# Top-k attention and SwiGLU: seven-product gate and value in the last two token blocks

## The chip, the cores and the metric

The kernel runs on one core of a Trainium2 chip. The metric is the device time of one execution in microseconds (us); lower is better. The engines are named as the profile names them: PE (matrix multiply) and PEld (its weight loads), DVE (vector), ACT (scalar), POOL (GpSimd), SP (which only issues DMAs here).

## What is computed

Two stages, all in fp32 (the inputs arrive as float64 for the weights):

```python
# attention: B, H, S, D = 8, 8, 576, 64
scores = q @ k.T / sqrt(D)
kth    = 32nd largest of each row
p      = softmax(where(scores >= kth, scores, -1e9))
x      = (p @ v) as (B*S, H*D) = (4608, 512)
# feed-forward: d_ff = 1536
g   = x @ w_gate                 # 512 -> 1536
val = x @ w_val                  # 512 -> 1536
out = (g * sigmoid(g) * val) @ w_out   # 1536 -> 512
```

## The kernel before, in words

**Attention.** The work of attention is cut into units: a unit is one batch, one tile of 128 query rows (the fifth tile has 64) and a pair of heads. For each unit PE makes the scores (L313, L299) into PSUM, ACT scales them into `sc`, DVE finds the 32 largest by four rounds of MAX8 and MATCH_REPLACE8 (L333, L337), POOL makes the exponent's bias (`shift`, L348), ACT makes the weights (`weigh`, L360 and L365), DVE inverts the sum (L379), and the rows are normalised, one head by ACT (L383) and one by POOL (L385). PE transposes them (`turn`, L399), ACT copies them out (L400), and PE multiplies with the values (`values`, L433), which ACT copies into `xT` (L449), transposed tokens.

**Feed-forward.** The 4608 tokens are cut into 18 blocks of 256 (`BLK`), numbered 0 to 17. Blocks 0 and 1 go another way (`feed_half`, L493, in halves of 128 tokens). For each later block `feed` makes twelve gate and twelve value tiles of 128 rows of d_ff by 256 tokens: four matmuls of 256 moving columns for each tile, one for each 128 of the 512 inputs (`product`, L577). Two tiles share one PSUM bank, of which the feed-forward has three. ACT takes the gate out as tanh(g/2) (L610), g/2 (L611) and adds one (L612), and POOL multiplies the two (L613); the value is copied by ACT (L617) and multiplied in by POOL (L618). The products with `w_out` are already made in the seven-product way from block 1 on: `quarter` (L643) is called seven times for a block, in the order 1, 7, 5, 6, 2, 4, 3, six matmuls of 256 columns each. Between the calls POOL makes the differences and sums of the two token halves of `h` that the next calls take as their stationary operand: `s32` (L650), a sum written into the late half (L658), `s32` again (L663), and the late half once more (L691). For call 7, `s32` of all six early rows must be there; for call 5, the sum of L658, which reads the late halves of all twelve rows. The text of the prediction calls the calls of `quarter` closing products, `s32` the half-differences and L658 the sums of halves.

**Weights.** `weights` is a generator. At each step it does a bit of the loading and rounding of `w_gate`, `w_val` and `w_out` to fp32 (`rounded`), and then, after the plain products of block 0 are done (`plain_done`), of the sums of `w_out` for the seven products (L170 to L186). It is advanced by `rounding`, which is called between DVE's steps of the selection (`dve`).

**Order.** The program's main loop runs over the units and writes the order of every engine's instructions by hand; each engine keeps this order. A generator such as `feed` yields a cost at each piece, and `pieces` calls it as long as a unit has credit, so that feed-forward matmuls stand between those of attention. Work that follows a product is put on two lists, `on_act` and `on_pool`, and written out at the next `flush`. After the last units there is only block 17, without attention beside it. All input loads and output stores are issued from SP, in order, but for three from ACT.

Tiles come from pools with a fixed number of buffers: a new tile takes the buffer that is free, and its first writer waits until the last reader of the old one is done. Those that the change touches: `w` (four buffers of 128 x 1024 x 4 bytes), `xT` (three), `gv` (three, for `half_g`, `val`, `p57`, `p16`), `h` (thirteen), and the three PSUM banks of `ps_f`.

Of the kernel before, what the change touches and what calls it, by code (L numbers as in the profile page):

```python
# [15 lines left out]
P = 128  # L16
# [9 lines left out]
def kernel(  # L26
# [59 lines left out]
    ffn = ctx.enter_context(tc.tile_pool(name="ffn", bufs=2))  # L86
    ps_t = ctx.enter_context(tc.tile_pool(name="ps_t", bufs=5, space=PSUM))
    ps_f = ctx.enter_context(tc.tile_pool(name="ps_f", bufs=3, space=PSUM))

    ident = consts.tile([P, P], FP32, name="ident")  # L90
    make_identity(nc, ident[:])
# [4 lines left out]
        nc.vector.memset(vt[:], 0.0)  # L96
        vlast.append(vt)
    wg = consts.tile([P, KC, DFF], FP32, name="wg")
    wv = consts.tile([P, KC, DFF], FP32, name="wv")
    wo = consts.tile([P, MC, DM], FP32, name="wo")  # L100

    def rounded(src, dst):
# [21 lines left out]
    def weights():  # L124


        pieces = []
        for f in range(0, DFF, WP):
            for src, dst in ((w_gate, wg), (w_val, wv)):
                for c in range(0, KC, 2):  # L130
                    rows = src[c * P : (c + 2) * P, f : f + WP]
                    pieces.append((
                        rows.rearrange("(c p) f -> p c f", p=P), dst[:, c : c + 2, f : f + WP]
                    ))
        for c in range(MC):
            pieces.append((
                w_out[c * P : (c + 1) * P].rearrange("p (c f) -> p c f", c=2),
                wo[:, c].rearrange("p (c f) -> p c f", c=2),
            ))
        pieces = [rounded(*p) for p in pieces]  # L140
        step = [0] * len(pieces)

        def upto(i, k):

            while 0 <= i < len(pieces) and step[i] < k:
                next(pieces[i], None)
                step[i] += 1


        lags = (5, 2, 0)  # L150
        for n in range(2 * len(pieces) + 4):
            for k, lag in enumerate(lags):
                if (n - lag) % 2 == 0:
                    upto((n - lag) // 2, len(lags) - k)
            ready[0] = max((n - 5) // 2 + 1, 0)
            early[0] = lambda: upto(n // 2, 2)
            yield
        early[0] = lambda: None


        add, sub = ALU.add, ALU.subtract
        lo, hi = slice(0, DM // 2), slice(DM // 2, DM)
        room = []
        for _ in range(3):
            t = ffn.tile([P, 4, DM // 2], FP32, tag="w", name="t", bufs=4)
            room += [t[:, 0:2], t[:, 2:4]]
        for m in range(0, MQ, 2):
            mm, nn = slice(m, m + 2), slice(MQ + m, MQ + m + 2)
            t3 = room.pop()
            nc.gpsimd.tensor_tensor(t3, wo[:, nn, hi], wo[:, mm, hi], sub)  # L170
            T[7] += [t3[:, i, :] for i in range(2)]
            yield
        while not plain_done:
            yield
        for m in range(0, MQ, 2):
            mm, nn = slice(m, m + 2), slice(MQ + m, MQ + m + 2)
            t1 = wo[:, mm, hi]
            nc.gpsimd.tensor_tensor(t1, t1, wo[:, mm, lo], sub)
            T[5] += [wo[:, m + i, hi] for i in range(2)]
            yield  # L180
            t2 = room.pop()
            nc.gpsimd.tensor_tensor(t2, wo[:, nn, hi], t1, sub)
            T[6] += [t2[:, i, :] for i in range(2)]
            yield
            t4 = conv.tile([P, 2, DM // 2], FP32, tag="size", name="t4", bufs=3)
            nc.gpsimd.tensor_tensor(t4[:], wo[:, nn, lo], t2, sub)  # L186
            T[4] += [t4[:, i, :] for i in range(2)]
            yield
        T[1] += [wo[:, m, lo] for m in range(MQ)]
        T[2] += [wo[:, MQ + m, lo] for m in range(MQ)]  # L190
        T[3] += [wo[:, MQ + m, hi] for m in range(MQ)]
        yield

    ready = [0]
    early = [lambda: None]
    plain_done = []
    T = {i: [] for i in range(1, 8)}
    weight = weights()

    def rounding(n):  # L200
# [270 lines left out]
    def flush(queue):  # L471
        while queue:
            queue.pop(0)()

    halves_of = {(kb, t): [] for kb in (0, 1) for t in range(2)}
    fed, told = [], []

    def feed_half(kb, t):

        while done.get(kb, 0) < NHP * P * (t + 1) or (t and (kb, 0) not in fed):  # L480
            yield None
        x = xT[kb]
        cols = slice(t * P, (t + 1) * P)
        hs = halves_of[kb, t]

        def product(w, g, then):
            ps = ps_f.tile([P, 4, P], FP32, tag="f", name="f")
            for i in range(4):
                m = 4 * g + i
                while not sure(4 * (m // 2) + (2 if w is wg else 4)):  # L490
                    yield None
                for kc in range(KC):
                    nc.tensor.matmul(  # L493
                        ps[:, i, :],
                        w[:, kc, m * P : (m + 1) * P],
                        x[:, kc, cols],
                        start=(kc == 0),
                        stop=(kc == KC - 1),
                    )
                if i == 3:  # L500
                    on_act.append(lambda: then(ps))
                if i % 2 == 1:
                    yield 1

        for g in range(MC // 4):
            while kb == 1 and (t or g) and t not in told:
                yield None
            h = ffn.tile([P, 4, P], FP32, tag="h", name="h", bufs=MS + 1)
            hs.append(h)

            def gate(ps, h=h):
                half = ffn.tile([P, 4, P], FP32, tag="gv", name="half_g", bufs=3)
                nc.scalar.activation(h[:], ps[:], AF.Tanh, scale=0.5)
                nc.scalar.mul(half[:], ps[:], 0.5)
                nc.scalar.add(h[:], h[:], 1.0)
                on_pool.append(lambda: nc.gpsimd.tensor_mul(h[:], h[:], half[:]))

            def value(ps, h=h):
                val = ffn.tile([P, 4, P], FP32, tag="gv", name="val", bufs=3)
                nc.scalar.copy(val[:], ps[:])  # L520
                on_pool.append(lambda: nc.gpsimd.tensor_mul(h[:], h[:], val[:]))

            yield from product(wg, g, gate)
            yield from product(wv, g, value)
        fed.append((kb, t))
        if kb == 0 and t == 1:
            xT.pop(0)
# [35 lines left out]
    def feed(kb):  # L563
# [7 lines left out]
        def product(w, s, then):  # L571
            ps = ps_f.tile([P, 2, BLK], FP32, tag="f", name="f")
            need(4 * s + (2 if w is wg else 4))
            for i in range(2):
                m = 2 * s + i
                for kc in range(KC):
                    nc.tensor.matmul(  # L577
                        ps[:, i, :],
                        w[:, kc, m * P : (m + 1) * P],
                        x[:, kc, :],  # L580
                        start=(kc == 0),
                        stop=(kc == KC - 1),
                    )
                if i == 1:
                    on_act.append(lambda: then(ps))
                yield 1
# [4 lines left out]
            "p (m t) -> p m t", t=P  # L591
        )

        def pair(m, t):

            if kb == 1:
                return halves_of[1, t][m // 4][:, m % 4 : m % 4 + 2, :]
            return hs[m // 2][:, :, late if t else first]
# [1 line left out]
        def one(m, t):  # L600
            return pair(m - m % 2, t)[:, m % 2, :]

        for s in range(MS if kb > 1 else 0):
            h = ffn.tile([P, 2, BLK], FP32, tag="h", name="h", bufs=MS + 1)
            hs.append(h)

# [11 lines left out]
                on_pool.append(lambda: nc.gpsimd.tensor_mul(h[:], h[:], val[:]))  # L618

            yield from product(wg, s, gate)  # L620
            yield from product(wv, s, value)
        o = ffn.tile([P, 2, DM], FP32, tag="o", name="o", bufs=1)
        while len(T[3]) < MQ:
            next(weight)
# [7 lines left out]
        def quarter(i, ps):  # L632
            for m in range(MQ):
# [11 lines left out]
                )  # L645
                if m % 3 == 2:
                    yield 0.75

        for s in range(MS // 2):
            nc.gpsimd.tensor_tensor(  # L650
                s32[:, 2 * s : 2 * s + 2], pair(2 * s, 0), pair(2 * s, 1), ALU.subtract
            )
        yield from quarter(1, y_ps[:, 0])
        flush(on_act)
        flush(on_pool)
# [34 lines left out]
        for s in range(MS // 2):  # L690
# [3 lines left out]
                s32[:, 2 * s : 2 * s + 2],  # L694
                ALU.subtract,
            )
        y_ps2 = ps_f.tile([P, DH], FP32, tag="f", name="y_ps")
        yield from quarter(2, y_ps2[:])

# [115 lines left out]
    def run(steps):  # L815
        for _ in steps:
            pass
# [23 lines left out]
    for n in range(NU + 3):  # L841
# [40 lines left out]
            ahead = fetch(3)  # L882
        if n < NHP:
            load_v(n)
        pieces(2)
        flush(on_act)
        dve(1)
        dve(1)
        if 0 <= n - TURN < NU:
            run(turn(n - TURN))  # L890

# [8 lines left out]
        run(norm)  # L900
        dve(1 if n < AHEAD else 2, beside=False)
        run(topk)
        pieces(6)
    while piece():
        pass
# [48 lines left out]
```

## Time and profile before

| | |
|---|---|
| median of 3 runs (lowest to highest) | 1763.05 us (1759.49 to 1763.68) |
| the profiled execution's own time | 1760.46 us |
| its span | 1758.7 us |
| PE busy | 1680.1 us, 96% of the span |
| DVE busy | 1475.0 us, 84% |
| ACT busy | 1263.0 us, 72% |
| POOL busy | 798.2 us, 45% |
| mean granted PE clock | 0.974 |
| DMA | 59.72 MB, mean 34 GB/s |

The times that the prediction works with are those of the profiled execution, counted from the start of its span. Block 16 (the last but one) runs from 1614.8 to 1686.0 us, beside the last units of attention, and block 17 from 1695.0 to about 1754.9 us. In a line of a timeline, the first number is the start, the second the length, "x16" the number of records merged, and a bracket holds the engine's idle time before the line and whom it waited for. An fp32 matmul whose result is a product (not a transpose) leaves two records, so that "x32" is sixteen instructions. In a line of busy times, the first number after the stretch is its length, then the busy time of PE, PEld, DVE, ACT and POOL, the granted clock, the DMA engines' share and GB/s. Busy times of PE are not the same as PE at its peak, since matmuls are pipelined; the distance between two starts is what one costs.

### The profile page before, as it was taken

What the parts mean: (1) busy time and instruction counts of PE and PEld (TensorE: products, weight loads), DVE (VectorE), ACT (ScalarE), POOL (GpSimd) and SP (SyncE); (2) the same over time, 40 slices, a digit from 0 to 9 for tenths busy, and PEclk for the clock granted to TensorE, in tenths of its full rate; (3) what the DMA queues carried; (4) which work ended last, traced back from release to release, by engine and by line L of the source; (5) the groups of instructions that cost most, each with busy time, mean ns of one, the idle gap of its engine ahead of it and who ended that gap; (6) DMA issues with size and microseconds to landing.
All of it is one profiled execution on the core that took longest, in us unless ns stands there. A gap on an engine that the chain in (4) does not pass through costs nothing.

```text
span 1758.7 us, 31764 instructions
## 1 busy us (share of the span) xinstructions
PE 1680.1 (96%) x11408; PEld 1404.4 (80%) x11408; DVE 1475.0 (84%) x3311; ACT 1263.0 (72%) x2901; POOL 798.2 (45%) x910
## 2 busy tenths in 40 slices
PE   5678999899999999999999999999999999999999
PEld 3467688688888788887888878887888888888887
DVE  6998898998898898898989888998988888998300
ACT  7898686778767677768677787777776777676531
POOL 4898534243353425352535324443434333535334
PEclk6698999899999999999999999999999999999999
DMA  7442120003000130002100030000300020000000
GB/s 206 133 120 85 28 70 1 13 1 84 15 13 1 23 75 1 13 1 63 35 13 1 13 71 27 1 13 17 81 1 13 1 57 15 13 1 13 1 13 12
DMA packets 109309, 59.72 MB, mean 34 GB/s; under 512 B 88544, under 2 KB 96992, under 8 KB 109152
## 3 DMA queue, kind: packets, MB, share of 16 engines
q1 hardware_dynamic: 108016, 57.37, 12.5%
q8 instruction: 90, 1.47, 0.4%
q14 instruction: 67, 0.55, 0.1%
q10 hardware_dynamic: 1136, 0.33, 0.1%
HBM read 48.23 MB, written 9.44 MB: 33 GB/s over the span
## 4 chain that ended last, share of the span: by engine, by line
PE 84%; DVE 8%; ACT 5%; POOL 1%; issue 1%; DMA 1%; SPq 0%; ACTq 0%; POOLq 0%
PE f L577 38%; PE x_ps L643 9%; PE av L433 9%; PE y_ps L643 7%; PE s L313 7%; PE etps L399 7%; DVE m L333 4%; DVE e L337 3%; PE f L493 3%; PE s L299 2%; ACT e L365 1%; PE kqps L266 1%; DVE size L120 1%; ACT e L360 1%; PE o_ps L545 0%
## 5 line engine op out<-in xcount | busy, mean ns | idle before, releaser
L333 DVE MAX8 m<-e 128x8 f32<-128x576 f32 x864 | 615.2, 748 | 3.1
L337 DVE MATCH_REPLACE8 e<-m,e 128x576 f32<-128x576 f32 x576 | 424.0, 743 | 0.0
L577 PE MATMUL f<-xT,wg 128*128 128x256 f32 x1536 | 353.5, 381 | 0.0
L577 PE MATMUL f<-xT,wv 128*128 128x256 f32 x1536 | 353.1, 380 | 0.0
L577 PEld LDWEIGHTS f<-xT,wg 128*128 128x128 f32 x1536 | 286.8, 190 | 44.4 <-issue 7.9
L577 PEld LDWEIGHTS f<-xT,wv 128*128 128x128 f32 x1536 | 287.1, 190 | 43.4 <-issue 6.8
L613 POOL TENSOR_TENSOR h<-h,half_g 128x512 f32<-128x512 f32 x96 | 122.5, 1276 | 338.3 <-ACT h L612 330.3
L365 ACT ACTIVATE e<-e,bias 128x576 f32<-128x576 f32 x288 | 221.2, 775 | 39.4 <-POOL bias L348 36.6
L399 PE MATMUL etps<-ident,e 128*128 128x128 f32 (+1 forms) x1312 | 181.8, 281 | 42.4 <-ACT sc L318 19.8
L337 DVE MATCH_REPLACE8 e<-m,sc 128x576 f32<-128x576 f32 x288 | 212.0, 743 | 0.0
L360 ACT ACTIVATE e<-sc,m 128x576 f32<-128x576 f32 x288 | 211.4, 787 | 0.0
L399 PEld LDWEIGHTS etps<-ident,e 128*128 128x128 f32 (+1 forms) x1312 | 154.4, 143 | 71.1 <-POOL e L385 18.0
L618 POOL TENSOR_TENSOR h<-h,val 128x512 f32<-128x512 f32 x96 | 122.5, 1276 | 195.1 <-ACT val L617 185.4
L333 DVE MAX8 m<-sc 128x8 f32<-128x576 f32 x288 | 203.4, 743 | 7.3 <-ACT sc L318 7.3
L318 ACT ACTIVATE sc<-s 128x288 f32<-128x288 f32 x512 | 167.3, 414 | 52.9 <-PE s L313 52.4
L385 POOL TENSOR_TENSOR e<-e,tot 128x576 f32<-128x576 f32 x140 | 160.9, 1153 | 80.2 <-DVE tot L379 66.2
L400 ACT COPY et<-etps 128x512 f32<-128x512 f32 (+1 forms) x448 | 183.5, 490 | 13.9 <-PE etps L399 13.7
L313 PE MATMUL s<-kqT 64*128 64x288 f32 x1024 | 174.0, 448 | 17.9 <-ACT sc L318 7.4
L378 DVE TENSOR_SCALAR tot<-tot 128x1 f32<-128x1 f32 x228 | 29.7, 147 | 170.4 <-ACT e L365 170.0
L433 PE MATMUL av<-et,v 128*64 128x128 f32 (+1 forms) x2560 | 159.7, 268 | 0.0
L313 PEld LDWEIGHTS s<-kqT 64*128 64x128 f32 x1024 | 96.6, 193 | 64.7 <-issue 23.7
L383 ACT ACTIVATE e<-e,tot 128x576 f32<-128x576 f32 x148 | 118.8, 803 | 35.5 <-DVE tot L379 35.2
(85 smaller groups left out, 2273.2 us busy)
## 6 DMA issues: line engine op xcount, KB each, us to landing
v<-in_v_dram SPq DMA_DIRECT2D x32, 256.0 KB, 3.3
kq_in<-in_k_dram SPq DMA_DIRECT2D x63, 128.0 KB, 2.8
kq_in<-in_q_dram SPq DMA_DIRECT2D x63, 128.0 KB, 3.2
w<-in_moe_w_gate_dram SPq DMA_DIRECT2D x12, 512.0 KB, 3.9
w<-in_moe_w_val_dram SPq DMA_DIRECT2D x12, 512.0 KB, 3.8
w<-in_moe_w_out_dram SPq DMA_DIRECT2D x12, 512.0 KB, 3.6
out_dram<-o SPq DMA_DIRECT2D x38, 128.0 KB, 2.4
out_dram<-o SPq DMA_DIRECT2D x16, 256.0 KB, 2.5
```

What stands on the lines that cost most here:

```text
L313: nc.tensor.matmul(ps[:, 0:half], slab[d, q0 : q0 + P], slab[d, k0 : k0 + half])
L318: nc.scalar.mul(sc[:, i * half : (i + 1) * half], ps[:, 0:half], scale)
L333: nc.vector.max(m[:, t, 8 * r : 8 * r + 8], cur[:, hs])
L337: nc.vector.match_replace(e[:, hs], m[:, t, 8 * r : 8 * r + 8], cur[:, hs], LOWEST)
L360: nc.scalar.activation(e[:, hs], sc[:, hs], AF.Prelu, bias=m[:, t, TOP_K - 1 : TOP_K], scale=-1.0, alpha=SMALL,)
L365: nc.scalar.activation(e[:, hs], e[:, hs], AF.Exp, bias=bias[:, t : t + 1], scale=-1.0 / SMALL, accum_out=tot[:, t : t + 1],)
L385: nc.gpsimd.tensor_tensor(e[:, hs], e[:, hs], tot[:, t : t + 1].to_broadcast([P, S]), ALU.mult)
L399: nc.tensor.transpose(ps[0:kl, c * P : (c + 1) * P], e[:, k0 : k0 + kl], ident[:])
L400: nc.scalar.copy(et[0:kl, c0 : c0 + cn, :], ps[0:kl, 0 : cn * P].rearrange("p (c j) -> p c j", c=cn),)
L433: nc.tensor.matmul(av[d, i, 0:ql], weights_, moving, start=c == (0 if last else J), stop=c == (J if last else J - 1),)
L577: nc.tensor.matmul(ps[:, i, :], w[:, kc, m * P : (m + 1) * P], x[:, kc, :], start=(kc == 0), stop=(kc == KC - 1),)
L643: nc.tensor.matmul(ps, lhsT, T[i][m], start=m == 0, stop=m == MQ - 1)
```

## The change

In blocks 16 and 17 (`QUICK = NBLK - 2`) the gate and the value are made together, in the Winograd form of Strassen's scheme. The weights are taken as a 2 x 2 matrix (gate above value, the first 256 inputs and the last 256), and the transposed tokens as one (first and last 256 inputs, first and last 128 tokens). Seven products take the place of eight, each of half the inputs and of 128 moving columns:

| product | stationary | moving |
|---|---|---|
| 1 | gate, first inputs (A11) | b11 |
| 2 | gate, last inputs (A12) | b21 |
| 3 | S4 = A12 - S2 | b22 |
| 4 | value, last inputs (A22) | t4 = b21 - t2 |
| 5 | S1 = A21 + A22 | t1 = b12 - b11 |
| 6 | S2 = S1 - A11 | t2 = b22 - t1 |
| 7 | S3 = A11 - A21 | t3 = b22 - b12 |

- The four sums of weights S1 to S4 are made once, by POOL, in 24 operations of 128 x 512 (six columns of 256 times four), at the end of the `weights` generator. Each is written to DRAM by a DMA from SP. They alternate between the two halves of one tile, `tx`, which is the fourth buffer of `w`.
- `w_val` is now held in two parts: the last 256 inputs in one constant tile, the first 256 in six tiles of 128 x 512 of a pool `ring`. When block 15 has read them, the six buffers serve for the stream: six chunks of 256 KB are loaded ahead of block 16, and after each of the products 6, 5, 7 and 3, which use two chunks, two more are asked for (`stream`), 48 in all.
- The four differences of tokens t1 to t4 are made by POOL into `tx`: four operations of 128 x 256 for a block. Those of block 16 stand in block 15, after L691; those of block 17 at the start of block 17.
- A block is worked in three groups of four rows of 128 of d_ff, each group in the order 1, 6, 2, 5, 7, 4, 3; a product is eight matmuls of 128 columns into one PSUM bank.
- ACT copies products 1, 5, 7, 4 and 3 out of PSUM; DVE adds products 6 and 2 to the copy of 1, two products later in the order. POOL makes the other additions: nine operations of 128 x 512 for a group, among them the products with the tanh. tanh and its scaling by 0.5 plus 0.5 are two operations of ACT for each half of the tokens; for the late half they come two products after product 3.
- `h` of these blocks has its token halves in tiles of their own, so that `quarter` reads them through a changed `pair`. `tick` and two flushes are added so that what is left after product 3 is written out during the first call of `quarter`.

The core of the diff (new functions shown whole where the text speaks of them):

```diff
+    ring = ctx.enter_context(tc.tile_pool(name="ring", bufs=DFF // WP))
+    dram = ctx.enter_context(tc.tile_pool(name="dram", bufs=1, space=bass.MemoryType.DRAM))
...
-    wv = consts.tile([P, KC, DFF], FP32, name="wv")
+    wv1 = [ring.tile([P, 2, WP], FP32, tag="r", name="wv1") for _ in range(DFF // WP)]
+    wv2 = consts.tile([P, KC - 2, DFF], FP32, name="wv2")
...
+        tx.append(ffn.tile([P, 4, 2, P], FP32, tag="w", name="tx", bufs=4))
+
+        def sums(i, c, in0, in1, op):
+            k = 0 if i in (1, 4) else 2
+            t = tx[0][:, k : k + 2].rearrange("p a b t -> p a (b t)")
+            nc.gpsimd.tensor_tensor(t, in0, in1, op)
+            d = dram.tile([P, 2 * WP], FP32, tag=f"s{i}_{c}", name=f"s{i}_{c}")
+            nc.sync.dma_start(d[:], t.rearrange("p c f -> p (c f)"))
+            S_[i][c] = d
+            return t
+
+        for c in range(DFF // WP):
+            cols = slice(c * WP, (c + 1) * WP)
+            a11, a12, a21, a22 = wg[:, 0:2, cols], wg[:, 2:4, cols], wv1[c][:], wv2[:, :, cols]
+            t = sums(1, c, a21, a22, add)
+            yield
+            t = sums(2, c, t, a11, sub)
+            yield
+            sums(4, c, a12, t, sub)
+            yield
+            sums(3, c, a11, a21, sub)
+            yield
...
+    def stream(n):
+        for _ in range(n):
+            if chunks:
+                _, i, c = chunks.pop(0)
+                t = ring.tile([P, 2, WP], FP32, tag="r", name="sw")
+                nc.sync.dma_start(t[:].rearrange("p c f -> p (c f)"), S_[i][c][:])
+                loaded.append(t)
+
+    def differences(x):
...
+        for d, in0, in1 in ((t1, b12, b11), (t2, b22, t1), (t3, b22, b12), (t4, b21, t2)):
+            nc.gpsimd.tensor_tensor(d, in0, in1, ALU.subtract)
+        return {1: b11, 2: b21, 3: b22, 4: t4, 5: t1, 6: t2, 7: t3}
+
+    ORDER = (1, 6, 2, 5, 7, 4, 3)
...
+        def later(out, in0, in1, op):
+            on_pool.append(lambda: nc.gpsimd.tensor_tensor(out[:, :], in0[:, :], in1[:, :], op))
+
+        def silu(h, g):
+            nc.scalar.activation(h[:], g[:, :], AF.Tanh, scale=0.5)
+            nc.scalar.activation(h[:], h[:], AF.Copy, bias=0.5, scale=0.5)
+            later(h, h, g, mult)
+
+        def follow(i, g, ps, t):
+            hf, hl = hs[2 * g], hs[2 * g + 1]
+            if i == 1:
+                t["a"] = tx[1][:, 0]
+                nc.scalar.copy(t["a"], ps[:])
+            elif i == 5:
+                t["b"] = copied("b", ps)
+            elif i == 7:
+                nc.scalar.copy(hl[:], ps[:])
+                later(hl, hl, t["u"], add)
+                later(t["u"], t["u"], t["b"], add)
+                later(t["b"], t["b"], hl, add)
+            elif i == 4:
+                v = copied("v", ps)
+                later(v, v, hl, add)
+                later(hf, hf, v, mult)
+            else:
+                g_late = copied("g", ps)
+                later(g_late, g_late, t["u"], add)
+
+                def end():
+                    silu(hl, g_late)
+                    later(hl, hl, t["b"], mult)
+
+                waiting.append([2, end])
+
+        def follow_dve(i, g, ps, t):
+            if i == 6:
+                t["u"] = tx[1][:, 1]
+                nc.vector.tensor_tensor(t["u"], ps[:], t["a"], add)
+            else:
+                nc.vector.tensor_tensor(t["a"], ps[:], t["a"], add)
+                waiting.append([1, lambda: silu(hs[2 * g], t["a"])])
+
+        for g in range(MC // G):
+            t = {}
+            for i in ORDER:
+                phase[0] += 1
+                flush_dve(2)
+                flush(on_act)
+                tick()
+                flush(on_pool)
+                ps = ps_f.tile([P, G, P], FP32, tag="f", name=f"p{i}")
+                own = [loaded.pop(0), loaded.pop(0)] if i in (3, 5, 6, 7) else None
+                for r in range(G):
+                    m = G * g + r
+                    for c in range(2):
...
+                        nc.tensor.matmul(
+                            ps[:, r, :], lhsT, moving[i][:, c, :], start=c == 0, stop=c == 1
+                        )
+                if own:
+                    stream(2)
...
+                yield 1
...
-        for s in range(MS if kb > 1 else 0):
+        if fast:
+            yield from quick(kb, x, hs)
+        for s in range(MS if 1 < kb < QUICK else 0):
...
         for s in range(MS // 2):
             nc.gpsimd.tensor_tensor(
                 s32[:, 2 * s : 2 * s + 2], pair(2 * s, 0), pair(2 * s, 1), ALU.subtract
             )
+        if fast:
+            flush(on_act)
+            flush(on_pool)
         yield from quarter(1, y_ps[:, 0])
...
+        if kb + 1 == QUICK:
+            stream(DFF // WP)
+        if QUICK <= kb + 1 < NBLK and done.get(kb + 1, 0) == NHP * BLK:
+            moving_of[kb + 1] = differences(xT[kb + 1])
```

## The prediction

> **What bounds the kernel now.** I read the busy times by stretch first, for the places where the change acts: the block before the last (1614.8 to 1686 us), the hand-over (to 1695) and the last block (to 1755). Columns: length, then busy time of PE, PEld, DVE, ACT, POOL, granted clock, DMA share, GB/s.
>
> ```profile
> 1614.80:1686.00 71.20, 71.20 (x412) 60.76 (x410) 27.42 (x61) 34.38 (x71) 31.84 (x37) 1.00 0.03 8
> 1686.00:1695.00 9.00, 6.39 (x91) 5.11 (x90) 0.32 (x2) 4.44 (x10) 1.27 (x1) 0.81 0.26 60
> 1695.00:1755.00 60.00, 59.85 (x280) 52.36 (x276) 0.97 (x3) 14.57 (x27) 26.78 (x28) 1.00 0.03 6
> ```
>
> PE has no gap in either block and POOL is under half busy: time taken from PE there is worth its full length until something else is late. The chain that ended last says the same; it holds only PE for the last 60 us:
>
> ```profile
> 1695.08 41.64 PE f L577 x192
> 1736.72 2.59 PE y_ps L643 x12
> 1739.31 5.18 PE x_ps L643 x24
> 1744.49 5.18 PE y_ps L643 x24
> 1749.67 5.19 PE x_ps L643 x24
> ```
>
> Next, the timeline of PE, for products of 128 moving columns (L493) and of 256 (L577). An instruction is two records, so x32 is 16 instructions and x16 is 8:
>
> ```profile
> 146.20 3.74 PE L493 MATMUL f<-xT,wg 128*128 128x128 f32 x32
> 149.77 3.74 PE L493 MATMUL f<-xT,wv 128*128 128x128 f32 x32
> ...
> 1702.02 3.62 PE L577 MATMUL f<-xT,wg 128*128 128x256 f32 x16
> 1705.47 3.62 PE L577 MATMUL f<-xT,wv 128*128 128x256 f32 x16
> ```
>
> Start to start: 3.57/16 = 0.223 us at 128 columns, 3.45/8 = 0.432 at 256. Half the columns cost 3.4% more than half.
>
> Then POOL, late in the last block (idle before it in brackets):
>
> ```profile
> 1738.26 1.27 POOL L618 TENSOR_TENSOR h<-h,val 128x512 f32<-128x512 f32 x1
> 1739.48 2.09 POOL L658 TENSOR_TENSOR h<-h 128x256 f32<-128x256 f32 x3
> 1741.53 2.09 POOL L663 TENSOR_TENSOR xT<-h 128x256 f32<-128x256 f32 x3
> ```
>
> A 128x512 operation takes 1.27 us and lets the next start after 1.23; 128x256 takes 0.73, pitch 0.69. One that waits for the operation just before it starts 0.08 after its end (L630 at 1747.83, 0.72 long, the next at 1748.63), so 1.35.
>
> Last, what a PE gap does:
>
> ```profile
> 1676.27 0.71 PE L399 MATMUL etps<-ident,e 128*128 128x128 f32 x5
> ...
> 1691.11 1.33 PE L399 MATMUL etps<-ident,e 128*128 128x128 f32 x5 [2.61 <-ACT e L383]
> ```
>
> After a 2.6 us gap the same five transposes took 1.33 instead of 0.71 us, and PE was slow to about 1694.5.
>
> **What the Trainium skill says.** "TensorE: Matmul & The Clock Gate", section Back-to-back issue gap, gives columns ÷ 2.4 GHz plus about 2.5 ns: a fixed part, so halved columns do not halve the time; the trace agrees (0.223 against 0.432). The same page, What's actually happening, has the clock at half after an idle window of some 3.4 us and for as long again; here 2.6 us sufficed, and the measurement decides. "GPSIMD Engine Reference", section 4.1 Engine selection, puts two-input elementwise work on POOL at about twice VectorE's time, and anything that touches PSUM elsewhere. For one unseen operation, a 128x512 add on DVE from PSUM, I take the price of "VectorE: DVE Perf Modes", the errata section: (N+151)/0.96, so an estimate of 0.69 us; it gives 424 ns at 256 columns, where L707 took 0.42.
>
> **Part 1, the saving.** Before, a block has 96 products of 256 columns: 41.44 us. After, 7 x 24 = 168 of 128 columns: 37.5 us (21 products of 1.786 us). Saved: 3.9 us in each of two blocks, 7.9 in all. The seven closing products of a block (2.59 each, 18.1) stay.
>
> **Part 2, POOL in the last block.** Before, 12 operations of 128x512 (L613, L618). After, each of three groups has nine: 9 x 1.23 = 11.1 us at best against 7 x 1.786 = 12.5 us of PE. Five of them wait for the one before (+0.12 each), and the late gate needs ACT (tanh, then scale: 0.60 + 0.09 + 0.63, with hand-overs 1.45) between two POOL operations: about 13.1 us a group. So POOL's latency exceeds PE's period. With the first product at 0: group 0 starts on POOL at 9.2 (product 5 ends at 7.1; copy, tanh, scale on ACT) and ends at 22.3, group 1 at 35.4. Group 2's first six operations run to 43.1, the three half-differences queued next to 45.1, then the add for the late gate to 46.4, ACT to 47.8, two products to 50.4, and the first sum of halves is there at 51.1.
>
> PE ends its products at 37.5 and the first closing product at 40.1. The second needs the half-differences (43.85): wait 3.7, end 46.4. The third needs the sums of halves (51.15): wait 4.7, end 53.7. Four more end at 64.1. Before: 41.5 + 18.1 = 59.6. So +4.5; half clock after the second gap adds some 3.4/2 = 1.7 (the first one's is mostly inside the wait): **+6.1**. Bounds +4.5 (no clock loss) and +9 (both, and POOL 1 us later a group). Even a POOL without backlog needs 0.6 + 1.27 + 1.45 + 2.6 + 0.7 = 6.6 us and the half-differences' 2.1 behind the last product, against two closing products (5.2 us) that cover it: 3.5 of the 3.9 saved are given back there alone.
>
> **Part 3, the block before the last.** Attention gives PE 71.2 - 41.4 - 18.1 = 11.7 us of other work, so products are slower than POOL; the same walk, with POOL's three normalisations and biases between, has products ending at 48.1, one PE wait of 0.6 (product 7 wants the buffer of product 6, which DVE frees after POOL's add), PE ready for the third closing product at 53.9 and the sums of halves at 58.3: wait 4.4, clock 1.7. The four differences of x (0.69 each, 2.75) are queued on POOL between L691 and L385, a normalisation that ends 0.27 us before transposes at 1613.85 take it: +2.0 more. Sum: -3.9 + 0.6 + 4.4 + 1.7 + 2.0 = **+4.8**, bounds 0 and +7.
>
> **Part 4, the weight sums.** 24 POOL operations of 1.29 us (31 us) between about 230 and 296 us, where POOL is busy some 25 us of 60. They alternate between two buffers, and each waits for the store of two before: 256 KB stores land in 2.5 us, so a buffer turns in 1.29 + 2.65, 12 turns 47 us. Walking POOL's queue with its other operations at their old ready times, it is 4.8 us late at 248, 8.2 late at 268 and 5.3 late here:
>
> ```profile
> 284.92 1.15 POOL L385 TENSOR_TENSOR e<-e,tot 128x576 f32<-128x576 f32 x1
> 286.03 0.20 POOL L348 TENSOR_TENSOR bias<-m 128x2 f32<-128x2 f32 x1
> ```
>
> The earlier ones have slack (267.26 feeds transposes at 280.69). This one has none: PE's transposes at 285.56 take it at once, and ACT's L365 already waited 1.64 us for the bias. DVE, 95 to 100% busy from 280 to 360, waits behind that exp. **+5.2**, bounds 0 (slack in the three score buffers) and +8.2.
>
> **Costed at nothing.** Stream: a pair of chunks is freed when its product ends and wanted four products later, 7.1 us; two issues of 0.6 and a landing of 3.3 (the v row, also 256 KB) are 4.5. Without that cover, PE would wait the excess at each of 9 refills. SP: 24 stores of 0.6 stand between loads wanted a batch later. ACT: 27 operations for 24, about 1.5 us in a 40% busy queue. DVE: six adds of 0.69 a block, half idle there.
>
> **Sum.** 5.2 + 4.8 + 6.1 = +16.1, on 1760.46 (span 1758.7 and 1.8 around it): 1776.6, say 1776. The median shown is 2.6 above that execution, the runs spread over 4.
>
> **Rivals.** (a) The sums are hidden: their lateness dies in the buffers ahead of DVE. For: PE waits over 7 us from 300 to 340 anyway; against: the zero slack at 285. 1760.5 + 10.9 = 1771. (b) The other side, faster: POOL delivers each block's last late halves within the 5.2 us of two closing products, so that PE never waits and the whole 7.9 us stays, the sums hidden too: 1752.5. It decides at 5.2 us behind the last product; the sum above is 8.7 without any backlog. Only operations much shorter than their rows would do it. (c) Little change: half of each wait hidden, no clock loss: about 1763. (d) The stream binds: were a pair to land 10 us after it is freed, 2.9 us at 9 refills of the last block, in place of part of POOL's wait: about 1790. Against it: DMA is 3% busy there.
>
> **Chances.** Forecast 0.55, (a) 0.27, (b) 0.04, (c) 0.09, (d) 0.05. About 0.3% (5.3 us) is what this measurement can tell from no change. Forecast, (d) and most of (a) are slower, 0.86; (c) and the rest of (a) are the same, 0.10; faster 0.04. Range: low end with sums 0, blocks +1 and +4.5, 1766; high end 8.2 + 7 + 9 with the runs' spread, 1787.
>
> **What would show it.** In the profile after: 37 to 38 us of seven-product work in the last block (right for part 1); PE waiting for POOL ahead of the second and third closing products of the last block, 3 to 5 us each, and ahead of the third one of the block before; POOL over 90% busy in the last 50 us; clock below 1.00 after those gaps; POOL 5 to 8 us late near 285 us, with PE or DVE behind it. PE waiting for a DMA in the last block would prove me wrong on the stream; closing products without gaps, on POOL altogether.

## The result and the profile after

The changed kernel takes **1783.41 us** (median of 4 runs, 1782.41 to 1785.01). The kernel before, on the same chip, took 1763.37 us (4 runs, 1759.49 to 1764.51). The ratio is 1.012, with a 95% interval of 1.0107 to 1.0132: slower by about 20 us, against 16 predicted. The profiled execution took 1783.08 us, with a span of 1781.3 and a mean clock of 0.967 (before: 0.974).

The places that the prediction looked at first, the same three stretches, now as long as they have become: block 16, the hand-over, block 17. Columns: length, busy time of PE, PEld, DVE, ACT, POOL, clock, DMA share, GB/s.

```profile
1621.60:1699.50 77.90, 71.69 (x562) 65.08 (x560) 32.13 (x69) 37.19 (x76) 53.76 (x57) 0.96 0.30 89
1699.50:1707.97 8.47, 5.86 (x91) 4.63 (x91) 0.60 (x3) 4.44 (x10) 2.18 (x3) 0.87 0.28 64
1707.97:1777.50 69.53, 62.92 (x422) 58.49 (x420) 5.02 (x9) 17.29 (x30) 47.47 (x46) 0.89 0.26 74
```

The first stretch begins with the transposes ahead of block 16, 1 us before its first product. Counted in the same way it took 72.1 us before, without a gap and at clock 1.00; it is 77.9 at 0.96 now, and PE is idle for 6 of them. In block 17 PE is idle for 6.6 of 69.5 us and the clock is 0.89. (PE counts as busy while it works at a low clock, so idle time is only a part of the loss.) DMA went from a share of 0.03 to 0.30 and 0.26 in the two blocks, and no wait of PE there ends on it.

The last stretch of the chain that ended last is now this; the columns are start, length, engine, result and line:

```profile
1753.29 2.05 POOL xT L836 x3
1755.34 1.23 POOL g L582
1756.59 0.64 ACT h L585
1757.25 0.64 ACT h L586
...
1758.02 1.27 POOL h L582
1759.36 1.26 POOL h L582
1760.63 0.69 POOL h L847
1761.36 5.49 PE x_ps L828 x12
```

PE's last gate and value product ended at 1747.8. From there until 1761.36 the path lies on POOL and, for the tanh, on ACT; only then on PE. The third closing product comes 13.6 us behind the last product. It takes 5.49 us on PE; the same line took 2.75 before. That POOL is behind with its work, and not only slow with each piece, is seen from ACT's copy of the last product:

```profile
1748.03 0.59 ACT L578 COPY g<-p 128x512 f32<-128x512 f32 x1 [1.20 <-POOL h L582]
```

This copy was done at 1748.6, and POOL took it up (`g` in the chain above) at 1755.3: it stood in POOL's queue for 6.7 us.

The timeline of PE shows the places where the two blocks lose time (in brackets the idle time before the line and its releaser):

```profile
1624.26 0.77 PE L439 MATMUL etps<-ident,e 128*128 128x128 f32 x5 [2.06 <-POOL e L425]
...
1683.07 5.49 PE L828 MATMUL x_ps<-wo,h 128*128 128x256 f32 x12 [4.05 <-POOL h L847]
...
1707.97 3.78 PE L642 MATMUL p<-xT,wg 128*128 128x128 f32 x16
1711.54 2.45 PE L642 MATMUL p<-tx,sw 128*128 128x128 f32 x16
...
1754.02 4.29 PE L828 MATMUL x_ps<-t,xT 128*128 128x256 f32 x12 [3.49 <-POOL xT L836]
1761.36 5.49 PE L828 MATMUL x_ps<-wo,h 128*128 128x256 f32 x12 [3.05 <-POOL h L847]
```

The waits are for POOL. The transposes behind the first one run at full speed. The closing products behind the other three are slow: 5.49 us twice, which is half speed, and 4.29. The first two products of block 17 are slow without a wait of their own (1.95 each later in the block): they inherit the low clock from the hand-over's gap of 2.61 us, which was there before the change too. The granted clock (third figure from the end) in stretches that are cut where it changes:

```profile
1681.85:1688.68 6.83, 5.61 (x13) 4.54 (x14) 0.00 (x0) 0.09 (x1) 4.58 (x7) 0.50 0.00 0
1688.68:1705.75 17.07, 14.46 (x116) 12.13 (x117) 2.11 (x7) 8.31 (x18) 8.52 (x12) 1.00 0.14 32
1705.75:1712.57 6.82, 6.82 (x55) 6.35 (x52) 0.00 (x0) 1.19 (x4) 2.09 (x3) 0.50 0.00 0
1753.53:1756.95 3.42, 2.93 (x7) 2.39 (x8) 0.00 (x0) 0.36 (x1) 3.03 (x4) 0.50 0.00 0
1760.36:1767.19 6.83, 5.83 (x14) 4.66 (x15) 0.00 (x0) 0.30 (x1) 4.36 (x7) 0.50 0.00 0
```

Three of the four low stretches last 6.8 us and one 3.4. The clock was 1.00 from 1688.68 to 1705.75, so that the low clock at the start of block 17 is not left over from block 16's wait.

The weight sums, last, where POOL's normalisation had no slack (it stood at 284.92, and the bias behind it at 286.03). Now POOL's timeline has

```profile
291.03 1.14 POOL L425 TENSOR_TENSOR e<-e,tot 128x576 f32<-128x576 f32 x1
292.13 0.19 POOL L388 TENSOR_TENSOR bias<-m 128x2 f32<-128x2 f32 x1
```

and PE's

```profile
287.17 1.56 PE L828 MATMUL x_ps<-t,xT 128*128 128x256 f32 x6 [1.82 <-POOL xT L836]
...
292.22 0.98 PE L439 MATMUL etps<-ident,e 128*128 128x128 f32 x5 [3.06 <-POOL e L425]
292.99 2.77 PE L828 MATMUL x_ps<-t,xT 128*128 128x256 f32 x6
```

Both brackets are new (1.8 and 3.1 us), and the third line is the half clock behind them: 2.77 us where 1.46 is usual. The first product of a later block starts at 340.25 instead of 332.48, and this lag stays between 7.7 and 7.8 us until 1612 us: nothing takes it back. 0.9 us of it is already there at 214 us, before the first weight sum has run. The kernels of the experiments, which are alike up to there, stand at -1.7 to +1.9 us at this place, so that this part is scatter.

Where the 22.6 us between the two spans lie, by PE's timeline: 0.9 before the sums, 6.9 at the sums, 5.8 in block 16, -0.6 in the hand-over, 9.6 in block 17.

### The profile page after: what moved, and what is told of

It is laid out like the page before. It is cut to its first block, busy times and chain, and to the rows that moved or that the text cites. A ratio compares the mean times of both kernels' runs of the same rounds, so it can differ in the third digit from the quotient of the medians.

```text
span 1781.3 us, 32585 instructions
## 1 busy us (share of the span) xinstructions
PE 1684.4 (95%) x11696; PEld 1414.8 (79%) x11696; DVE 1484.4 (83%) x3323; ACT 1267.6 (71%) x2907; POOL 870.9 (49%) x972
## 4 chain that ended last, share of the span: by engine, by line
PE 76%; POOL 8%; ACT 8%; DVE 4%; issue 2%; DMA 1%; SPq 0%; POOLq 0%; ACTq 0%
PE f L756 32%; PE av L473 9%; PE x_ps L828 9%; PE s L353 7%; PE y_ps L828 6%; PE etps L439 6%; POOL h L582 2%; ACT e L405 2%; DVE m L373 2%; DVE e L377 2%; PE s L339 2%; PE f L672 1%; PE kqps L306 1%; POOL tx L213 1%; ACT e L400 1%
## 5 line engine op out<-in xcount | busy, mean ns | idle before, releaser
L756 PE MATMUL f<-xT,wg 128*128 128x256 f32 x1344 | 309.8, 381 | 0.0
L756 PE MATMUL f<-xT,wv 128*128 128x256 f32 x1344 | 309.7, 380 | 0.0
L756 PEld LDWEIGHTS f<-xT,wg 128*128 128x128 f32 x1344 | 250.7, 190 | 39.0 <-issue 7.3
L756 PEld LDWEIGHTS f<-xT,wv 128*128 128x128 f32 x1344 | 250.8, 190 | 38.6 <-issue 6.8
L798 POOL TENSOR_TENSOR h<-h,half_g 128x512 f32<-128x512 f32 x84 | 107.3, 1277 | 286.6 <-ACT h L797 278.7
L803 POOL TENSOR_TENSOR h<-h,val 128x512 f32<-128x512 f32 x84 | 107.3, 1277 | 181.3 <-ACT val L802 171.7
```

Source lines behind the costliest of these rows:

```text
L756: nc.tensor.matmul(ps[:, i, :], weight_of(w is wg, kc, m), x[:, kc, :], start=(kc == 0), stop=(kc == KC - 1),)
```

## The experiments

My theory after the result: the mechanisms are those of the prediction (POOL's backlog at the end of both blocks, POOL's queue at the sums, the differences ahead of a normalisation), and the part that I had too small is the clock, which falls to half behind most of the gaps. Rivals: the slow products are slow because their operands arrive piece by piece; or the latency of the chain, not POOL, makes the waits; or stores and streaming do. Line numbers differ by a few from kernel to kernel. All medians are beside runs of the kernel before on the same chip (1761.2 to 1762.9). The changed kernel was timed beside 1763.4, so a difference from its 1783.41 holds up to 2 us of difference between chips; the ratios do not.

| kernel | median, us | ratio to before (95%) |
|---|---|---|
| sums only | 1769.81 | 1.0046 (1.0033 to 1.0059) |
| no sums | 1779.06 | 1.0093 (1.0079 to 1.0107) |
| last block only | 1776.88 | 1.0081 (1.0067 to 1.0095) |
| fill in the waits | 1778.38 | 1.0083 (1.0065 to 1.0100) |
| sums spread | 1779.32 | 1.0091 (1.0078 to 1.0105) |
| VectorE in the last block | 1775.13 | 1.0066 (1.0054 to 1.0079) |
| closing products reordered | 1775.47 | 1.0080 (1.0061 to 1.0098) |
| differences late | 1784.67 | 1.0126 (1.0112 to 1.0141) |
| four mends | 1760.70 | 0.9989 (0.9981 to 0.9997) |
| mends, VectorE in block 16 | 1757.93 | 0.9974 (0.9965 to 0.9984) |
| the same with a fill in the hand-over | 1755.13 | 0.9966 (0.9952 to 0.9980) |
| before with that fill | 1760.46 | 0.9995 (0.9987 to 1.0003) |

**The weight sums alone, and everything but them.**

```diff
-    QUICK = NBLK - 2
+    QUICK = NBLK
```

> Blocks 16 and 17 run the old way; the 24 weight sums are still made on POOL and stored, and nobody reads them. The sums theory (they come ahead of attention's work on POOL near 290 us, PE waits and then runs at half clock, and the lag is never made up) expects what the two traces show between 283 and 340 us: +6.9 us over the kernel before, so about 1770. The rival, that this lag would be made up later if the last two blocks were the old ones, expects 1763 to 1765. Predicted for this part beforehand: +5.2 (1768.6).

Measured 1769.81, 7.1 above the kernel before. The trace has the same two waits (1.71 and 3.06 us), and the lag stays to the end: 6.8 us of it arise between 239 and 406 us, where the changed kernel has 6.9. That the sums would be hidden, the prediction's rival (a), is out. The counterpart:

```diff
-            nc.gpsimd.tensor_tensor(t, in0, in1, op)
-            nc.sync.dma_start(d[:], t.rearrange("p c f -> p (c f)"))
+            t = in1
+            nc.sync.dma_start(d[:].rearrange("p (c f) -> p c f", c=2), t)
```

> The changed kernel without the 24 POOL operations that make the weight sums: plain slices of the weights are stored in their place (same 24 stores, same streaming, the output is not the reference's). If POOL's operations make the lag: 1783.4 - 6.9 = 1776.5. If the stores make it (SP's queue or DMA traffic): no change, 1783.

Measured 1779.06: 4.4 less than the changed kernel, not 6.9. The waits near 290 us are gone, and at 332 us the lag is 0.2, so it is POOL's part and not the traffic of the stores that made it. (POOL's waits for a free half of `tx`, 6.1 us in five places, went together with its operations; the run does not part the two.) But by 685 us the trace has a lag of 1.9. One place makes it, and it teaches something. The kernel before, there:

```profile
610.78 0.33 PE L259 MATMUL kqps<-ident,kq_last 128*128 128x128 f32 x1 [2.00 <-ACT et L400]
...
612.42 1.04 PE L433 MATMUL av<-et,v 128*64 128x128 f32 x16
```

and the kernel without sums:

```profile
610.97 0.33 PE L298 MATMUL kqps<-ident,kq_last 128*128 128x128 f32 x1 [2.00 <-ACT et L439]
...
612.65 1.93 PE L472 MATMUL av<-et,v 128*64 128x128 f32 x16
```

The same gap of 2.00 us, at the same place in the same instructions; once it costs nothing, once the products after it take nearly twice as long and PE loses 1.7 us. The same happens at the start of block 16: behind the wait of 2.06 us the first product takes 3.17 us here and 1.95 in the changed kernel, and 1.6 us are lost. Such luck in two places is more than the 2.7 us by which the two estimates of the sums (7.1 and 4.4) differ. By the medians I put the sums at 4 to 7 us; in the seven traces that have them all in this place, 5.4 to 8.4 us of lag arise there.

**The last block alone.**

```diff
-    QUICK = NBLK - 2
+    QUICK = NBLK - 1
```

> The new way in the last block alone. By the trace block 16 costs 5.8 us and block 17 about 9.0 with the hand-over (9.6 - 0.6), so 1783.4 - 5.8 = 1777.6 and, seen from before, 1763.4 + 6.9 + 0.9 + 9 = about 1780. As predicted beforehand: -4.8. If the blocks are not separate (the low clock at the start of block 17 is left over from block 16's stall), the last block would be cheaper by some 2.3 us more: 1775.

Measured 1776.88. Seen from the changed kernel the parts add within a microsecond (6.5 us for block 16 against 5.8 in the trace). Seen from the kernel before they fall short: 14.2 us against 15.9 (6.9 at the sums, 9.0 in the hand-over and the last block). In this execution the hand-over and block 17 cost 6.8 us and not 9.0, most of it because the low clock behind the hand-over's gap was shorter: the first product of block 17 takes 2.96 us (3.78 in the changed kernel) and the second runs at full speed. There was no stall in block 16 here, so the low clock at the start of block 17 does not need one. The PE timeline in the last block has

```profile
1747.96 2.86 PE L828 MATMUL x_ps<-t,xT 128*128 128x256 f32 x12 [3.50 <-POOL xT L836]
1755.30 5.03 PE L828 MATMUL x_ps<-wo,h 128*128 128x256 f32 x12 [4.48 <-POOL h L847]
```

After a gap of 3.50 us the second closing product ran at full speed here (2.86); in the changed kernel it took 4.29 after 3.49. The wait that follows is 4.48 instead of 3.05: longer by just what the product before it was shorter. POOL sets when the third product starts; a slow second product is hidden by that wait, and a slow third one is not.

**Filling the waits.** 12 products that nobody reads, ahead of the closing products that wait:

```diff
+            for i in range(n):
+                nc.tensor.matmul(ps[:, 0:P], wg[:, 0, 0:P], wg[:, 1, 0:P], start=True, stop=True)
```

> The changed kernel with 12 unused 128x128 products (12 x 0.223 = 2.7 us) on PE ahead of the third closing product of both blocks and of the second of the last block, so that the 3 to 4 us waits there shrink to some 0.4 to 1.4 us. Clock theory (a wait of 3 us costs a further 2.7 because the next product runs at half clock): closing products back from 5.3-5.5 to 2.6-2.8, about -2.7 for each of the two third ones and -1 to -1.5 for the second one, so 1776 to 1777. Rival (these products are slow because their operands come late from POOL, piece by piece): no change, 1783; below it nothing is added, since the fill lies inside the waits.

Measured 1778.38, 5.0 less; in its profiled execution the lag behind the sums happened to be 3.7 us and not 7.8 (it was 1.7 us ahead when they began), so the median alone would prove little. What matters are the third closing products of both blocks:

```profile
1682.32 2.86 PE L834 MATMUL x_ps<-wo,h 128*128 128x256 f32 x12 [1.35 <-POOL h L853]
...
1757.85 2.86 PE L834 MATMUL x_ps<-wo,h 128*128 128x256 f32 x12 [1.81 <-POOL h L853]
```

They start as late as POOL lets them and still take 2.86 us, not 5.49. Late operands do not make a product slow; PE's idle time before it does. This is the run that settles the clock.

**Spreading the sums.**

```diff
-            yield
+            yield from [None] * 8
```

(after each of the four sums of a column)

> Same changed kernel, but the 24 weight sums are handed to POOL an eighth as often (one for every eight turns of the generator, so over some 400 us and not over 65). If the sums cost because they crowd POOL's queue where block 1 and the weights' own sums already fill it: the lag at the first later product falls to that without sums, so -4.4 (the run without sums) to -7.1 (the run with sums alone): 1776 to 1779. If any weight sum ahead of a normalisation costs, wherever it stands: no gain, 1783 or more.

Measured 1779.32, as much gain as leaving the sums out (1779.06). The waits at 287 and 292 us are gone (0.41 is left at 311). In the trace 1.2 us of lag arise between 239 and 406 us and not 6.9 (1.2 to 2.7 in the later kernels with the same spread). So it was mostly the crowding at that place and not the work.

**VectorE for the last block.**

```diff
-            on_pool.append(lambda: nc.gpsimd.tensor_tensor(out[:, :], in0[:, :], in1[:, :], op))
+            on_pool.append(lambda: side.tensor_tensor(out[:, :], in0[:, :], in1[:, :], op))
...
+        side = nc.vector if kb == NBLK - 1 else nc.gpsimd
```

(`side` also makes the half-differences, sums of halves and what follows)

> The changed kernel with every elementwise sum and product of the last block's gate, value and closing halves on VectorE in place of POOL; ACT and PE do the same as before. If POOL's backlog is the cause: the waits of 3.5 and 3.05 us before the second and third closing products fall to under 1 us and the half clock behind them (4.3 and 5.5 us products) goes with them, -8 to -10, so 1773 to 1775. Rival (the latency of the chain product, ACT, sum, ACT, products is what counts, on whichever engine): only the wait before the second product goes, the one before the third stays near 3 with its half clock, -4, 1779.

Measured 1775.13, 8.3 less. The wait for the half-differences is gone and that for the sums of halves is 0.15 us:

```profile
1752.72 2.86 PE L830 MATMUL x_ps<-wo,h 128*128 128x256 f32 x12 [0.15 <-DVE h L849]
```

On VectorE the 128x512 operation takes 0.69 us against POOL's 1.27, and the first sum of halves is there about 5.4 us behind the last product instead of 13.5. Two closing products cover 5.2. So the prediction's rival (b) had its point of decision right; POOL was the engine that could not meet it. The run makes each operation and the queue of them shorter at once, so it shows that POOL is the cause and does not part the two.

**Reordering the closing products.** Number 2 reads early halves only:

```diff
         yield from quarter(7, x_ps[:, 1])
+        if fast:
+            y_ps2 = ps_f.tile([P, DH], FP32, tag="f", name="y_ps")
+            yield from quarter(2, y_ps2[:])
```

> The changed kernel, in blocks 16 and 17 with the closing product that reads early halves only (number 2) moved ahead of number 5, which waits for POOL's sums of halves. Same work. Theory (PE has nothing to do until POOL is done, and each gap of 3 us or more costs another 2.7 in clock): waits of 4.05 and 3.05 shrink by the product's 2.6 to about 1.5 and 0.5, -5.2, and most of the clock's 5.4 goes with them: 1773 to 1778. Rival (the next product, number 6, or the PSUM buffers wait instead): 1781 to 1783.

Measured 1775.47, 7.9 less. The wait in block 16 fell from 4.05 to 1.42 us and the product after it takes 2.86. In the last block it fell to 1.88, and that product took 4.23. I had missed a new wait: the last closing product now waits 1.06 and 1.65 us for the late halves of L886, which POOL makes after its output sums and which number 2 had covered until then.

**The differences of block 16 at its start.**

```diff
-        if QUICK <= kb + 1 < NBLK and done.get(kb + 1, 0) == NHP * BLK:
-            moving_of[kb + 1] = differences(xT[kb + 1])
```

> The changed kernel without the early call for the differences of block 16's inputs: they are made at the start of block 16's own gate and value. Theory: the 2.06 us wait of attention's transposes for POOL's normalisation near 1624 us goes, and product 6 (which needs two differences, 1.4 us) hides behind product 1 (1.8 us): -2, so 1781.4. Rival: product 6 waits for the differences in its place, 1783.

Measured 1784.67: the rival was right. The 2.06 us wait at 1624 is gone, and product 6 waits 3.17 us for the differences. POOL's timeline says why:

```profile
1625.06 1.27 POOL L815 TENSOR_TENSOR o<-o,p 128x512 f32<-128x512 f32 x1 [2.72 <-ACT o L923]
1626.28 0.73 POOL L542 TENSOR_TENSOR tx<-xT 128x256 f32<-128x256 f32 x1
```

In its new place the first difference stands behind block 15's last output sum, which waits 2.72 us for ACT. The right place is between: behind the normalisation, ahead of this sum.

**The four mends together.** Spread sums; VectorE in the last block; number 2 early, with L880's operations ahead of product 6 in both blocks; and

```diff
         yield from quarter(4, x_ps2[:, 1])
+        if QUICK <= kb + 1 < NBLK and done.get(kb + 1, 0) == NHP * BLK:
+            moving_of[kb + 1] = differences(xT[kb + 1])
```

> The four mends at once: weight sums an eighth as often; block 17's elementwise sums on VectorE; closing product 2 ahead of 5 in both blocks, and the last half-sums issued ahead of product 6; the differences of block 16's inputs placed on POOL behind the normalisation and the first output sum of block 15, where POOL was idle for 2.7 us. If the parts add: 1783.4 - 4.1 (spread) - 8.3 (VectorE) - 5.3 (block 16's waits 4.05 -> 1.4 with their half clock 2.7) - 2.1 (differences) = 1763.6, level with the kernel before; the 7.9 us saved on PE would then be eaten by what is left: 1.4 us in block 16, some clock loss, some lag of the sums. If the half clock merely falls on other products when one gap is closed, less adds: 1768 to 1770.

Measured 1760.70 against 1762.01 for before. The differences now fill the place where POOL stood idle, and the wait at 1624 is gone. One wait for POOL is left after block 15: 1.44 us in block 16.

```diff
-        side = nc.vector if kb == NBLK - 1 else nc.gpsimd
+        side = nc.vector if fast else nc.gpsimd
...
+                end_side = nc.vector if g == MC // G - 1 else side
```

(`end_side` makes the late gate of the last group)

> As the run with all four mends, and in block 16 the closing half-sums and the late gate of the last group on VectorE as well. If POOL's speed is what is left there (1.4 us wait before product 5): that wait falls to under 0.5 us, -1 to -1.4 against the run with the four mends. Rival: VectorE carries attention's selection there and is 39% busy; its sums stand behind an instruction that waits for ACT, and the wait stays or grows, +0 to +4.

Measured 1757.93, 2.8 less; the 1.44 us wait is gone entirely, and the rest of the gain is within what executions differ by. PE has no gap in either block. From the last closing product of block 15 to that of block 17 it takes 135.0 us (before: 140.9), though the hand-over's low clock costs some 1.5 us more here than in that execution of before (3.0 against 1.5, by the two fills below). Both together are 7.5 of the 7.9 us that part 1 promised.

**A fill in the hand-over**, 11 unread products in the wait for the last exponentials, in the best kernel and in the kernel before:

```diff
+        if n == NU - 1:
+            for _ in range(11):
+                nc.tensor.matmul(idle[:, 0:P], wg[:, 0, 0:P], wg[:, 1, 0:P], start=True, stop=True)
```

> The best kernel so far (four mends, and VectorE for block 16's closing sums) with 11 unused 128x128 products (2.45 us) in the hand-over's 2.6 us wait for the last head pair's exp and scale. In that kernel the stretch from the wait's end to the third product of the last block took 9.1 us where full clock gives 5.9. Clock theory: -3 us (1755). Rival (the low clock comes anyway, from the attention products of 64 columns, or the fill delays the transposes): 0 to +1 (1758 to 1759).

> The kernel before with the same fill: what the hand-over's clock is worth without the change. There the stretch from the wait's end to the first product took 3.9 us where full clock gives 2.3. Clock theory: -1.6 (1760.5). Rival: 0 (1762).

Measured 1755.13 and 1760.46. In the first, PE's timeline after the fill is

```profile
1689.50 0.77 PE L443 MATMUL etps<-ident,e 128*128 128x128 f32 x5 [0.15 <-ACT e L423]
...
1691.95 2.05 PE L648 MATMUL p<-xT,wg 128*128 128x128 f32 x16
```

From the wait's end to the block's third product it takes 6.1 us instead of 9.1: the low clock is gone. What that is worth, the medians do not settle: this kernel is 6.0 us below the kernel before on its chip, the one without the fill was 4.1 below on another, and the intervals of the two ratios overlap. In the kernel before the same stretch to its first product fell from 3.9 to 2.4 us in the trace, but the ratio of 0.9995 (0.9987 to 1.0003) does not tell that from nothing. With the fill in both, on one chip, the changed and mended kernel is 5.3 us faster (1755.13 against 1760.46). In the two traces its last two blocks, with the hand-over, take 132.0 us against 139.5, counted as above: 7.5 us are gained there, and the spread sums cost 2.7.

## Why the prediction was right, and where its size was off

- **Sign, place and range** held: 1783.4 lies in 1766 to 1787, and PE waits for POOL at each place that was named.
- **Part 1, 3.9 us saved in a block: right.** In block 17 a product costs 1.786 us start to start, but for the two slow ones. With the mends and the fill, 7.5 us of the 7.9 are kept in the two blocks, and 5.3 in the median.
- **Part 2, the walk of POOL's queue in the last block: right to half a microsecond.** Predicted: sums of halves 13.65 us behind the last product; measured 13.5. Waits 3.7 and 4.7 predicted; 3.5 and, with the slow product inside it, 4.5 measured. The reason given, backlog, is seen in POOL's queue (the late gate stood in it for 6.7 us), and VectorE's run shows that POOL is the cause.
- **Part 3: right.** The wait for the displaced normalisation was 2.06 us (2.0), that for the sums of halves 4.05 (4.4), and the late PSUM buffer cost about 0.4 (0.6).
- **Part 4, the sums: 5.2 predicted, 6.9 in the trace, 4 to 7 by the medians.** With the 0.9 us of earlier lag taken off, POOL's normalisation is 5.2 us late at 291, as walked (5.3), and PE's two waits are 4.9 us. The rest, 1.8, is clock.
- **The step that was mis-sized is the clock**: "half clock after the second gap adds some 3.4/2 = 1.7 (the first one's is mostly inside the wait)". That the first one's is hidden was right. Outside the waits, the trace has 1.8 us at the sums, 2.9 in block 16 (the third closing product and a little of the fourth), 5.3 in block 17 (3.0 there, 2.3 in its first two products), less 0.6 in the hand-over: 9.4 against 3.4. Two errors are in it. The 1.7 lets the low clock last 3.4 us, of which half is lost. The low stretches around the two third closing products last 6.8 us, 5.6 and 5.8 of them with PE at work, so that 2.9 and 3.0 us are lost. And I gave no clock loss to the sums or to the first products of block 17; the low clock of the hand-over was in the profile of before, and I did not ask what it would fall on.
- The difference of 6.0 in the clock and 0.9 before the sums, less 0.4 in the waits, make the 6.5 us between the sum (1776.6) and this execution (1783.1).
- **The stream, costed at nothing: right.** No wait of PE in the two blocks ends on a DMA.
- Two small slips in the sums: 4.5 and 1.7 make 6.2, not 6.1, and the low end of the range takes block 16 at +1, though its bound is 0. Neither bears on the result.
- **Wrong in what would show it:** POOL was not over 90% busy at the end; it was 83% from 1717 to 1764 us. ACT's tanh and scale leave it idle for 1.47 us in each group, and yet POOL and ACT together carry the path. A share of one engine was the wrong sign to name.

## What to carry to other kernels

Work taken from the bounding engine is worth its length only if the engines that follow it can deliver the last piece within the cover that is left; here that cover was 5.2 us, POOL needed 13.5 and VectorE 5.4. A gap in PE is to be priced with the slow work behind it, here from nothing to 4.1 us for gaps of 1.8 to 4.5 us, unless another wait follows that hides it. When an operation moves in a queue, look for the instruction in that queue that itself waits, and place it between the one that is urgent and the one that is blocked.

## What was not expected of the hardware

- **The clock behind a gap is a matter of the execution.** Gaps of 3.45 to 3.50 us before the second closing product were followed by 2.86 us in two kernels and by 4.26 to 5.49 in four; gaps of 1.84 and 1.88 us before the third by 2.86 and 4.23; the gap of 2.00 us at 611 us by nothing in seven traces and by some 1.7 us lost in seven, and kernels that are alike up to there stand on both sides. Behind the hand-over's 2.61 us the low clock cost 1.5 us in the kernel before, 3.0 in two others and 4.1 in the kernel with the four mends, where it lasted some 10.3 us. "TensorE: Matmul & The Clock Gate", What's actually happening, says that the clock is decided over a free-running window of some 3.4 us; that fits gaps of the same length ending differently, and low stretches of 3.4, 6.8 and 10.3 us. Its full idle window does not: 1.9 us sufficed here at times, and the measurement decides.
- One price held closely: VectorE took 0.69 us for the 128x512 add from PSUM, for which the prediction took an estimate of 0.69 from "VectorE: DVE Perf Modes", the errata section. It took 0.69 for the same from SBUF; POOL takes 1.27.
